# A decode step of two layers, twice: the row mean is carried by an extra column of wo and w2

## The chip, the cores and the metric

The kernel runs on one core of a Trainium2 chip. The metric is the device time of one execution in microseconds (us). The core has TensorE (PE in the profile; PEld is its weight load), VectorE (DVE), ScalarE (ACT), GpSimd (POOL) and SyncE (SP), which issues all transfers here.

## The reference

Eight batch rows, one token each, go through attention, a feed-forward part, the same attention again and the same feed-forward part again. Each has a residual and takes the normalised row:

```python
def _layernorm(x, axis=-1, eps=1e-5):
    m = jnp.mean(x, axis=axis, keepdims=True)
    v = jnp.var(x, axis=axis, keepdims=True)
    return (x - m) / jnp.sqrt(v + eps)
x = x + _A_ref(_layernorm(x), k_cache, v_cache, wq, wo)   # q = xn @ wq; softmax(q k^T / 16) v; @ wo
x = x + _B_ref(_layernorm(x), w1, w2)                     # silu(xn @ w1) @ w2
```

and so a second time. D is 448, there are 16 query heads and 8 key heads of 256, the last 1024 positions of K and V are used, and the hidden size of B is 1792. All is bf16. K and V of a batch are 8.4 MB, read once and kept for both attentions; the weights wq, wo, w1, w2 (3.7, 3.7, 1.6 and 1.6 MB) stay in SBUF.

The mean enters each product only through the row sums of the weights: (x - m) @ W is x @ W minus m times the column sums of W. The kernel before uses this; the change does not.

## The kernel before

**Order.** The kernel is a list of tasks, each with an engine, reads and writes (tiles and PSUM banks), an estimated duration and a priority. `Plan.schedule` plays them through in time with the constants at lines 12 to 30 (latencies, `OCC` durations by name, `HOLD`, `PE_SCALE`, and `BIAS`, which shifts the urgency of single kinds of task) and so fixes one order for each engine; `Plan.emit` writes it out with semaphore waits. Engines run their order strictly, so a task that waits holds everything behind it on its engine. SP's order is that in which the loads are listed.

**Loads.** x, wq, K of batch 0 (eight slots), wo, V of batch 0, w1, w2, then K and V of batches 1 to 7. There are 29 slots of 512 KB; a load into a used slot waits until the second attention has read it (`pump`). wo and w2 lie in SBUF as rows of 448 columns for each chunk of 128 input rows.

**Start** (`start_rows`, from line 522). x is turned into columns; the statistics of all 8 rows are taken (`stats8`); one product with wq gives all q of the first attention and, from a ninth column of ones (`xb0[:, :, NB]`, line 387), the column sums `csq`; these times the negative mean are added. `sums_w1` (line 558) gives w1's column sums `cs1` with 56 matmuls, once.

**One batch** (`layer1`, `layer2`). K is transposed in place on DVE (line 877, 16 operations), scores are 128 matmuls for both attentions (line 598), softmax follows. `x_init` (line 716) puts the residual row, as columns, in bank YB. P times V: four kv heads by rows (line 655), four by columns (line 684). `wo_part` (line 726) multiplies seven heads with wo into bank XB, four partial rows; `fold` (line 748) copies them with ACT (L750) and sums and turns them into columns in YB by five matmuls (`to_cols`, line 495), while two filler matmuls (`keep`, line 743) run on PE; the last head goes straight to columns (`wo_cols`, line 735). Then `chain` (line 755):

- `xcols`: DVE copies the row to `xbt` (L697). `stats`: four matmuls with ones give the sum (L701), four the sum of squares (L703); DVE makes nmean, vn, var4 (L706, L708, L711), POOL the power -1/2 (L713, `rhalf`).
- 56 matmuls with w1 (L488); DVE adds `cs1` times nmean (vpos, L762); ACT tanh (L766), DVE hT (L768); 14 matmuls with w2 (L771) into XB; `fold` again; `xcols` to `x2b` (L697); `stats` again.
- `maskr` on DVE (L779); two halves of q: 16 matmuls with wq (L784), copy on ACT (qrow, L789), turn (L792), qT2 on DVE with `csq` (L795), spread (L577) and masked (qbd, L581).

The second attention follows, beside the first attention of the next batch; its results of all batches wait in `oT2`. The end (`final_wo`, `final_rows`, from line 803) multiplies them with wo for all 8 rows, folds, takes `stats8`, w1, the `cs1` correction (L823, L826, L828), tanh and w2.

Of the kernel before, what the change touches and what calls it, by code (L numbers as in the profile page):

```python
# [18 lines left out]
OCC = {"dve:KT": 0.635, "dve:max": 0.35, "dve:maskr": 0.16, "dve:nmean": 0.10, "dve:vn": 0.15, "dve:var4": 0.15,  # L19
       "dve:vpos": 0.17, "dve:hT": 0.12, "dve:xb": 0.10, "dve:oTev": 0.10, "dve:qT2": 0.16, "dve:qbd": 0.36,  # L20
# [3 lines left out]
HOLD, PE_SCALE = 0.664, 1.032  # L24
BIAS = {"dve.KT.a": 22.4, "pe.S0.0.a": -78.2, "dve.max.a": 23.1, "pe.PV0.0.0.a": -52.9, "dve.oTev.a": 42.5,
        "pe.PV0.1.0.a": -21.9, "pe.PV0.1.1.a": 34.2, "dve.xb.b": 61.8, "dve.nmean.b": 76.2, "dve.vn.b": 130.7,
        "dve.var4.b": 69.1, "pe.w1.b": -131.8, "dve.vpos.b": 70.6, "dve.hT.b": 26.1, "dve.maskr.b": 46.5,
        "dve.qT2.b": 102.1, "dve.qbd.b": 99.0, "pe.S1.0.b": -54.5, "dve.max.b": 66.3, "dve.mT.c": 39.4,
        "pe.l.c": 48.6, "pe.PV1.0.0.c": 53.0, "pe.PV1.0.1.c": 55.7, "pe.PV1.0.2.c": 50.5, "pe.PV1.0.3.c": 51.6,
        "pe.oT.c": -34.2, "pe.PV1.1.1.c": 94.7, "pe.PV1.1.2.c": -48.5}  # L30
# [220 lines left out]
def bass_interleave_layers__sliding_block_cached__dense_activation_silu__decode_kernel(  # L251
# [18 lines left out]
    XC = 5  # L270

# [5 lines left out]
    wo_sb = sb("wo_sb", [P, NCH * D], BF16)  # L277
    w1_sb = sb("w1_sb", [P, 3 * F + F2], BF16)
    w2_sb = sb("w2_sb", [P, FC * D], BF16)
# [4 lines left out]
    deps_sb = sb("deps_sb", [P, 1], F32)  # L284
# [6 lines left out]
    xb0 = sb("xb0", [P, XC, NB + 1], BF16)  # L291
    x2b = sb("x2b", [P, XC, NB], BF16)
    csq = sb("csq", [P, NCH], F32)
    cs1 = sb("cs1", [P, FC], F32)
# [11 lines left out]
    nmean = sb("nmean", [P, 1], F32)  # L306
    vn = sb("vn", [P, 1], F32)
# [3 lines left out]
    rowb = qrow[:, 0:D]  # L311
    cols_b = sb("cols_b", [P, 3], BF16)
    ones4, zero_b = cols_b[:, 0:1], cols_b[:, 1:2]
    ones_b = cols_b[:, 2:3].broadcast_to([P, P])
    fold8 = sb("fold8", [P, NB], BF16)
    xbt = sb("xbt", [P, XC], BF16)
    vpos = sb("vpos", [P, FC], F32)
# [10 lines left out]
    big8 = e1f.bitcast(F32)  # L328
    z8 = q0f.bitcast(F32)[:, 0:FC * NB]
    th8 = e0f.bitcast(F32)[:, 0:FC * NB]  # L330
    hT8 = q1f[:, 0:FC * NB]
    xbt8 = sb("xbt8", [P, XC, NB], BF16)
    xrow = q1f[0:NB, 0:D]
# [6 lines left out]
    C_XF = 256  # L340
# [34 lines left out]
    dve(lambda e: e.memset(deps_sb[:], D * EPS), [], ["deps"], 0.08, -99)  # L375
# [11 lines left out]
    dve(lambda e: e.tensor_copy(xb0[:, :, NB], mask5[:]), M5, ["xb0_1"], 0.1, -98)  # L387
    for q in range(4):
        dve(lambda e, q=q: e.tensor_copy(fold8[32 * q:32 * q + 32, :], ident[32 * q:32 * q + 32, 32 * q:32 * q + NB]),
            ["ident"], [("fold8", q)], 0.08, -98)  # L390
        dve(lambda e, q=q: e.memset(mask[32 * q:32 * q + 32, :], 0.0), [], [("mask", q)], 0.08, -98)
        dve(lambda e, q=q: e.memset(mask[32 * q:32 * q + 32, q:q + 1], 1.0), [], [("mask", q)], 0.08, -98)
# [10 lines left out]
    SEL_R = [("sel", i) for i in range(4)] + [("mask", i) for i in range(4)]  # L403
# [23 lines left out]
    def load_wo():  # L427
        dma(lambda e: e.dma_start(wo_sb[:].rearrange("p (c n) -> p c n", n=D),
                                  A_wo.rearrange("(c p) n -> p c n", p=P)), ["wo"], HD * D * 2, "wo", rate=380e3)
# [71 lines left out]
    def stats8(xp, reads, prio):  # L501
# [7 lines left out]
               for c in range(KC)]  # L509
# [4 lines left out]
        dve(lambda e: e.tensor_scalar(nmean8, s1, -1.0 / D, None, op0=ALU.mult), bk(STB), [("qbd", 0, 1)], 0.17, prio)  # L514
        dve(lambda e: e.tensor_tensor(vn8, s1, nmean8, ALU.mult), bk(STB) + [("qbd", 0, 1)], [("qbd", 0, 1)], 0.17, prio)
        dve(lambda e: e.tensor_tensor(vn8, s2, vn8, ALU.add), bk(STB) + [("qbd", 0, 1)], [("qbd", 0, 1)], 0.17, prio)
        dve(lambda e: e.tensor_scalar(vn8, vn8, D * EPS, 4.0 / D, op0=ALU.add, op1=ALU.mult), [("qbd", 0, 1)], [("qbd", 0, 1)],
            0.12, prio)
# [3 lines left out]
    def start_rows(prio):  # L522
# [3 lines left out]
            for c in range(XC)], H8 + ["ident"], bk(YB), (NB, 1), prio)  # L526
        dve(lambda e: e.tensor_tensor(xb0[:, :, 0:NB], xp[:, 0:XC * NB].rearrange("p (c b) -> p c b", b=NB),
                                      mask5[:].unsqueeze(2).broadcast_to([P, XC, NB]), ALU.mult),
            bk(YB) + M5, ["xb0"], 0.2, prio)
        stats8(xb0[:, :, 0:NB], ["xb0"], prio)  # L530
        N9 = NB + 1
        pe(proj(YB, 0, range(NCH), wq_l, 16, lambda i: xb0[:, i, :], N9),
           ["xb0", "xb0_1"] + WQ_R, bk(YB), (N9, 1), prio, "q1")
        yv = bank[YB][:, 0:NCH * N9].rearrange("p (c n) -> p c n", n=N9)
        dve(lambda e: e.tensor_copy(csq[:], yv[:, :, NB]), bk(YB), ["csq"], 0.2, prio)
        t = big8.rearrange("p (c b) -> p c b", b=NB)
        dve(lambda e: e.tensor_tensor(t, csq[:].unsqueeze(2).broadcast_to([P, NCH, NB]),
                                      nmean8.unsqueeze(1).broadcast_to([P, NCH, NB]), ALU.mult),
            ["csq", ("qbd", 0, 1)], B8, 0.35, prio)
# [18 lines left out]
    def sums_w1(prio):  # L558
        pe(proj(STB, 0, range(FC), w1_l, 7, lambda i: xb0[:, i, NB:NB + 1], 1),
           ["xb0_1"] + W1_R, bk(STB), (CW, 1), prio, "cs1")  # L560
        dve(lambda e: e.tensor_copy(cs1[:], bank[STB][:, 0:FC * CW:CW]), bk(STB), ["cs1"], 0.2, prio)


    def q_blocks1(b, prio):
        for k2 in range(2):
# [5 lines left out]
                reads=[("q1s", b // 4)] + SEL_R, writes=[("qbd", 0, k2)], dur=0.65, prio=prio, name="qbd1")  # L571

    def q_blocks(layer, qi, k2, qrow, q_reads, prio):

        lb = LB[layer]
# [3 lines left out]
            sel[:, c, :], qrow.rearrange("p (k r a) -> p k a r", k=4, r=2), start=True, stop=True) for c in range(4)]  # L579
        pe(fns, q_reads + SEL_R, bk(lb), (16, 1), prio, "qsel")  # L580
        dve(lambda e: e.tensor_tensor(  # L581
            qbd[qi][:, 4 * k2:4 * k2 + 4, :, :].rearrange("p k c (q r) -> p (k c) q r", r=2),
            qs.rearrange("p (n r) -> p n r", r=2).unsqueeze(2).broadcast_to([P, 32, 4, 2]),
            maskr[:].unsqueeze(1).unsqueeze(3).broadcast_to([P, 32, 4, 2]), ALU.mult),
            bk(lb) + ["maskr"], [("qbd", qi, k2)], 0.43, prio, "qbd")
# [110 lines left out]
    def xcols(dst, key, prio):  # L696
        dve(lambda e: e.tensor_copy(dst, bank[YB][:, 0:XC]), bk(YB), [key], 0.17, prio, "xb")  # L697
# [248 lines left out]
```

## Time and profile before

| | |
|---|---|
| time of the runs | median 283.28 us of 3 (283.14 to 284.43) |
| the profiled execution | 283.31 us; its span 281.5 us |
| PE, PEld, DVE, ACT, POOL busy | 203.1, 119.2, 155.1, 51.4, 22.6 us |
| matmuls | 4406, as many weight loads |
| transfers | 78.29 MB, mean 278 GB/s |
| granted TensorE clock, mean | 0.859 |

The span is from the first to the last instruction. Busy time of PE contains the pipelining of matmuls; the chain of waits goes back from the last instruction, at each step to what released it. "issue" in it is time in which the engine waited for nothing that the profile shows. SPq is SP's own queue. L and a number is a line of the kernel before.

### The profile page before, as it was taken

To read this page: it belongs to the slowest core of one execution; us is meant where nothing else is said; L and a number is where in the kernel's file an instruction comes from. 1 tells how busy PE (TensorE), PEld (TensorE's weight loads), DVE (VectorE), ACT (ScalarE), POOL (GpSimd) and SP (SyncE) were. 2 spreads that over 40 slices of the span, in tenths; PEclk is the share of its full clock that TensorE was granted. 3 is DMA by queue.
4 is the path that set the end of the run, shared out by engine and by line. 5 is a ranking of instruction groups with operands and counts; after the bars stand their busy time and mean duration, and the time that the engine had idled before them with its cause. 6 is when DMAs were issued, how large, how long until landed. Compare 5 with 4: busy or idle time off the path is not lost.

```text
span 281.5 us, 9739 instructions
## 1 busy us (share of the span) xinstructions
PE 203.1 (72%) x4406; PEld 119.2 (42%) x4406; DVE 155.1 (55%) x480; ACT 51.4 (18%) x119; POOL 22.6 (8%) x41
## 2 busy tenths in 40 slices
PE   1040649686697977988787978789877987985853
PEld 0040315533363555356524643555354535743430
DVE  6279220187556947693777477646763766224122
ACT  2000020020321141214122202311231123221111
POOL 1200100020000200020010002000200020000020
PEclk9999975595797999799979978995898799999575
DMA  6999999999999499949995997799679956000000
GB/s 250 357 409 384 372 349 359 376 407 354 361 407 364 130 356 410 357 142 393 401 329 189 398 384 246 225 409 375 192 237 407 377 182 220 8 2 2 2 0 1
DMA packets 50153, 78.29 MB, mean 278 GB/s; under 512 B 2225, under 2 KB 41025, under 8 KB 49729
## 3 DMA queue, kind: packets, MB, share of 16 engines
q1 hardware_dynamic: 50112, 77.68, 77.7%
q8 instruction: 34, 0.56, 0.8%
q14 instruction: 7, 0.05, 0.0%
HBM read 77.67 MB, written 0.01 MB: 276 GB/s over the span
## 4 chain that ended last, share of the span: by engine, by line
PE 58%; SPq 14%; DVE 13%; issue 5%; ACT 4%; DMA 3%; POOL 1%; ACTq 0%; DVEq 0%
PE bank L655 9%; SPq L455 9%; PE bank L598 8%; PE bank L784 6%; PE bank L488 6%; PE bank L743 5%; PE bank L684 5%; PE bank L726 4%; PE bank L771 4%; DMA w_sb<-in_B_w_dram 3%; DVE mseg L604 3%; DVE slot L877 3%; SPq L449 2%; SPq L443 2%; PE bank L735 1%
## 5 line engine op out<-in xcount | busy, mean ns | idle before, releaser
L877 DVE STREAM_TRANSPOSE slot<-slot 128x512 uint32<-128x512 uint32 x128 | 84.9, 691 | 9.9 <-DMA slot<-in_A_k_cache_dram 9.4
L598 PE MATMUL bank<-slot,qbd 128*8 128x256 bf16 x1024 | 40.3, 299 | 7.3 <-DVE mg L611 4.1
L655 PE MATMUL bank<-slot,pT_sb 128*2 128x256 bf16 x768 | 28.3, 291 | 4.3 <-ACT pT_sb L627 3.4
L598 PEld LDWEIGHTS bank<-slot,qbd 128*8 128x8 bf16 x1024 | 22.9, 89 | 17.8 <-DVE mseg L604 5.2
L713 POOL TENSOR_TENSOR rhalf<-var,nhalf 128x1 f32<-128x1 f32 x16 | 8.7, 542 | 204.1 <-DVE var L711 204.1
L618 ACT ACTIVATE e_sb<-bank,mb 128x256 bf16<-128x256 f32 x32 | 14.1, 471 | 55.1 <-DVE mb L614 55.1
L743 PE MATMUL bank<-sel,cols_b 128*128 128x480 bf16 x56 | 21.4, 461 | 2.6 <-DVE vpos L762 2.6
L655 PEld LDWEIGHTS bank<-slot,pT_sb 128*2 128x2 bf16 x768 | 16.3, 86 | 10.7 <-ACT pT_sb L627 5.0
L690 DVE TENSOR_TENSOR oT<-bank,rl_sb 128x4 bf16<-128x4 f32 x32 | 5.2, 161 | 27.4 <-PE bank L684 27.4
L684 PEld LDWEIGHTS bank<-pT_sb,slot 128*128 128x128 bf16 x512 | 15.1, 98 | 11.0 <-issue 10.3
L684 PE MATMUL bank<-pT_sb,slot 128*128 128x2 bf16 x512 | 17.2, 164 | 3.6 <-issue 2.7
L604 DVE TENSOR_REDUCE mseg<-bank 128x1 f32<-128x256 f32 x32 | 13.5, 423 | 10.1 <-PE bank L598 9.0
L488 PE MATMUL bank<-xbt,w_sb 128*128 128x32 bf16 (+1 forms) x504 | 15.2, 180 | 5.0 <-issue 4.6
L784 PE MATMUL bank<-wq_sb,x2b 128*1 128x512 bf16 x256 | 16.9, 384 | 2.2 <-DVE x2b L697 2.2
L488 PEld LDWEIGHTS bank<-xbt,w_sb 128*128 128x128 bf16 x504 | 14.0, 99 | 5.5 <-issue 5.1
L726 PE MATMUL bank<-wo_sb,oT 128*1 128x448 bf16 x224 | 15.6, 420 | 0.5 <-DVE oT L668 0.3
L636 DVE TENSOR_REDUCE l_sb<-bank 128x16 f32<-128x64 f32 x16 | 3.5, 221 | 20.1 <-PE bank L631 20.1
L623 PE MATMUL bank<-ident,e_sb 128*128 128x128 bf16 x64 | 6.7, 232 | 10.9 <-ACT e_sb L618 10.9
L789 ACT ACTIVATE qrow<-bank 128x512 bf16<-128x512 f32 x16 | 9.6, 597 | 23.0 <-PE bank L784 14.6
L662 ACT ACTIVATE e_sb<-bank 128x256 bf16<-128x256 f32 x24 | 9.2, 383 | 22.2 <-PE bank L655 22.2
L566 POOL TENSOR_TENSOR qbd<-q1s,mask 128x256 bf16<-128x256 bf16 x16 | 9.8, 613 | 21.2 <-DVE q1s L554 20.0
L771 PE MATMUL bank<-w_sb,hT 128*1 128x448 bf16 x112 | 11.4, 502 | 0.0
(122 smaller groups left out, 190.0 us busy)
## 6 DMA issues: line engine op xcount, KB each, us to landing
slot<-in_A_k_cache_dram SPq DMA_DIRECT2D x64, 512.0 KB, 10.6
slot<-in_A_v_cache_dram SPq DMA_DIRECT2D x64, 512.0 KB, 9.3
wo_sb<-in_A_wo_dram SPq DMA_DIRECT2D x1, 3584.0 KB, 26.0
wq_sb<-in_A_wq_dram SPq DMA_DIRECT2D x3, 1024.0 KB, 6.8
w_sb<-in_B_w_dram SPq DMA_DIRECT2D x1, 1568.0 KB, 13.0
w_sb<-in_B_w_dram SPq DMA_DIRECT2D x1, 1344.0 KB, 11.5
wq_sb<-in_A_wq_dram SPq DMA_DIRECT2D x2, 256.0 KB, 10.0
w_sb<-in_B_w_dram SPq DMA_DIRECT2D x2, 112.0 KB, 10.0
```

The lines of the kernel that those rows point to most:

```text
L455: dma(lambda e: e.dma_start(slots[s][:, :].rearrange("v (j n) -> v j n", j=4), src.rearrange("j (v uh) d -> v j (uh d)", uh=2)), [("slot", ...
L488: fns.append(lambda e, o=o, i=i, r=r: e.matmul(bank[bank_i][:, col + (o - outs[0]) * n:col + (o - outs[0] + 1) * n], lhs(o, i), r.broadcas ...
L598: fns.append(lambda e, cb=cb, par=par, j=j, kvh=kvh, kv=kv: e.matmul(bank[sc][32 * j:32 * j + 8, k2 * 256:(k2 + 1) * 256], qbd[qi][:, kvh, ...
L604: dve(lambda e: e.tensor_reduce(mseg[layer][:, k2:k2 + 1], bank[sc][:, k2 * 256:(k2 + 1) * 256], AX.X, ALU.max, negate=True), bk(sc), [("m ...
L618: act(lambda e, k2=k2: e.activation(e_sb[ei][:, k2, :, :].rearrange("p uh (jj ul) -> p uh jj ul", ul=4), bank[sc][:, k2 * 256:(k2 + 1) * 2 ...
L655: fns.append(lambda e, q=q, uh=uh, j=j, vv=vv: e.matmul(bank[ob][32 * j:32 * j + 2, c0:c0 + DH], pT_sb[ei][:, k2 * 2 + uh, j * 8 + 2 * q:j ...
L684: fns.append(lambda e, a=a, q=q, uh=uh: e.matmul(bank[vb][:, c0 + 2 * a:c0 + 2 * a + 2], vs[:, (2 * q + uh) * DH + a * P:(2 * q + uh) * DH ...
L726: fns.append(lambda e, i=i, c=c, kvh=kvh: e.matmul(bank[XB][32 * c:32 * c + 1, 0:D], oT1[:, i % 2, i // 2:i // 2 + 1], wo_sb[:, i * D:(i + ...
L743: pe([lambda e: e.matmul(bank[YB][:, 32:512], zero_b.broadcast_to([P, P]), sel[:].rearrange("p c m -> p (c m)")[:, 0:480], start=False, st ...
L771: pe([lambda e, f=f: e.matmul(bank[XB][32 * (f % 4):32 * (f % 4) + 1, 0:D], hT[:, f:f + 1], w2_sb[:, f * D:(f + 1) * D], start=(f < 4), st ...
L784: pe([lambda e, j=j, c=c, k2=k2, wb=wb: e.matmul(bank[wb][32 * j:32 * j + 1, :], x2[:, xcol(c, k2):xcol(c, k2) + 1], wq_sb[:, c * HD + ((4 ...
L877: dve(lambda e, v=v: e.transpose(v, v), [("slot", s)], [("slot", s)], 0.67, prio, "KT")
```

## The change

wo and w2 get a row pitch of 450 columns in SBUF (`DP`); column 448 holds minus the row sum over 448. `row_sums` makes it on the chip after the weights have landed: groups of rows in turn on DVE (one reduce of 4 or 5 rows and a scale) and on ACT (one copy with an accumulated sum for each row, and a copy). All products with wo wait for wo's eight groups, all with w2 for w2's four. w2 is loaded ahead of wo instead of behind w1.

The partial rows so have a 449th column, the negative mean of what is folded in. A sixth matmul of `to_cols` spreads it over all partitions into column 5 of YB; `wo_cols` gets four matmuls for it and `x_init` a second one with the low part of the mean (`xl0`). `xcols` adds that column to the row and masks it, in one operation of DVE, so `xbt` is centred. The sum matmuls, nmean, vn, vpos, `cs1`, `csq` and `sums_w1` go; var4 is an activation, as are maskr and a copy that keeps the row and its mean in `x2b`; the scale 2/16 moves into `mask`. tanh and hT read w1's bank. The second filler pair writes XB and reads wq. In the start, x is centred and split in a high and a low part (16 columns for q in place of 9, summed by one reduce). In the end the mean is a bf16 column (`nm8`), added and masked by two operations; the correction shrinks to one multiplication, and one matmul puts the mean back. The planner's constants are new.

```diff
-HOLD, PE_SCALE = 0.664, 1.032
-BIAS = {"dve.KT.a": 22.4, ...
+HOLD, PE_SCALE = 0.368, 1.013
+BIAS = {"pe.S0.0.a": -30.6, "dve.max.a": -4.8, "pe.PV0.0.2.a": -33.7, "pe.wo.a": 11.0, "pe.PV0.1.1.a": 56.1,
+        "pe.PV0.1.2.a": 10.4, "pe.keep.b": -44.7, "pe.wq.b": 14.6, "act.qrow.b": -18.2, "pe.S1.0.b": -29.4,
+        "dve.mT.c": -116.1, "pe.l.c": -24.2, "pe.oT.c": -8.5, "pe.PV1.1.0.c": -30.8, "pe.PV1.1.3.c": 37.4,
+        "pe.wo8.c": -80.4}
...
     def load_w2():
-        dma(lambda e: e.dma_start(w2_sb[:].rearrange("p (c n) -> p c n", n=D),
+        dma(lambda e: e.dma_start(w2_sb[:].rearrange("p (c n) -> p c n", n=DP)[:, :, 0:D],
...
-    WO_R = ["wo"]
-    W2_R = ["w2"]
+    WO_R = ["wo"] + [("wo_s", g) for g in range(8)]
+    W2_R = ["w2"] + [("w2_s", g) for g in range(4)]
+
+    def row_sums(w, key, groups, prio):
+
+        for g, (i0, i1) in enumerate(groups):
+            n = i1 - i0
+            row = sums[:, (8 if key == "w2" else 0) + g, :]
+            view = w[:, i0 * DP:i1 * DP].rearrange("p (c n) -> p c n", n=DP)
+            if g % 2 == 0:
+                dve(lambda e, view=view, n=n, row=row: e.tensor_reduce(row[:, 0:n], view[:, :, 0:D], AX.X, ALU.add,
+                                                                       negate=True),
+                    [key], [("sums", key, g)], 1.94, prio, "rsum")
+                dve(lambda e, view=view, n=n, row=row: e.tensor_scalar(view[:, :, D], row[:, 0:n], 1.0 / D, None,
+                                                                       op0=ALU.mult),
+                    [("sums", key, g)], [(key + "_s", g)], 0.15, prio)
+            else:
+                for i in range(i0, i1):
+                    act(lambda e, i=i, i0=i0, row=row: e.activation(
+                        qrow[:, 0:D], w[:, i * DP:i * DP + D], ACTF.Copy, scale=-1.0 / D,
+                        accum_out=row[:, i - i0:i - i0 + 1]), [key], ["rowb", ("sums", key, g)], 0.75, prio, "rsum")
+                act(lambda e, view=view, n=n, row=row: e.activation(view[:, :, D], row[:, 0:n], ACTF.Copy),
+                    [("sums", key, g)], [(key + "_s", g)], 0.22, prio)
...
+        fns.append(lambda e: e.matmul(bank[bank_i][:, col + XC * nb:col + (XC + 1) * nb],
+                                      row[:, D:D1].broadcast_to([P, P]), rhs, start=False, stop=True,
+                                      skip_group_check=True))
         pe(fns, reads, bk(bank_i), shape, prio, name)
...
-    def xcols(dst, key, prio):
-        dve(lambda e: e.tensor_copy(dst, bank[YB][:, 0:XC]), bk(YB), [key], 0.17, prio, "xb")
...
+    def xcols(prio):
+        dve(lambda e: e.scalar_tensor_tensor(out=xbt[:], in0=bank[YB][:, 0:XC], scalar=bank[YB][:, XC:XC + 1],
+                                             in1=mask5[:], op0=ALU.add, op1=ALU.mult), bk(YB) + M5, ["xbt"], 0.23, prio,
+            "xb")
+
+    def stats(bi, col, prio):
+        s2 = bank[bi][:, col:col + 1]
+        pe([lambda e, c=c: e.matmul(s2, xbt[:, c:c + 1].broadcast_to([P, P]), xbt[:, c:c + 1],
                                     start=(c == 0), stop=(c == KC - 1)) for c in range(KC)],
...
+        act(lambda e: e.activation(var4[:], s2, ACTF.Identity, bias=eps4[:, 0:1], scale=4.0 / D), bk(bi) + ["eps4"],
+            ["var4"], 0.25, prio, "var4")
...
+        for i in range(4 * kvh, 4 * kvh + 4):
+            fns.append(lambda e, i=i: e.matmul(
+                bank[YB][:, XC:XC + 1], wo_sb[:, i * DP + D:i * DP + D1].broadcast_to([P, P]),
+                oT1[:, i % 2, i // 2:i // 2 + 1], start=False, stop=True, skip_group_check=True))
...
-        dve(lambda e: e.scalar_tensor_tensor(out=vpos[:], in0=cs1[:], scalar=nmean[:, 0:1], in1=y1,
-                                             op0=ALU.mult, op1=ALU.add),
-            bk(YB) + ["cs1", "nmean"], ["vpos"], 0.23, prio, "vpos")
-        keep(2, prio)
-        act(lambda e: e.activation(th[:], vpos[:], ACTF.Tanh, scale=rhalf[:, 0:1]), ["vpos", "rhalf"], ["th"], 0.31,
+        act(lambda e: e.activation(th[:], y1, ACTF.Tanh, scale=rhalf[:, 0:1]), bk(YB) + ["rhalf"], ["th"], 0.31,
             prio, "tanh")
+        keep(2, prio, XB)
...
+        xcols(prio)
+        act(lambda e: e.activation(x2b[:, :, b], bank[YB][:, 0:XC + 1], ACTF.Copy), bk(YB), [("x2b", b)], 0.25, prio,
+            "x2b")
+        stats(LB[1], C_ST, prio)
+        act(lambda e: e.activation(maskr[:], mask[:], ACTF.Copy, scale=rhalf[:, 0:1]), ["rhalf"] + MASK_R, ["maskr"],
+            0.22, prio, "maskr")
...
+            dve(lambda e, k2=k2: e.tensor_copy(qT2[:, 16 * k2:16 * k2 + 16], bank[lb][:, C_QT:C_QT + 16]),
...
+        dve(lambda e: e.tensor_copy(nm8[:], x8[:, XC * NB:]), bk(YB), ["nm8"], 0.17, prio)
+        xcf = big8[:, 0:XC * NB].rearrange("p (c b) -> p c b", b=NB)
+        dve(lambda e: e.tensor_tensor(xcf, x8[:, 0:XC * NB].rearrange("p (c b) -> p c b", b=NB),
+                                      nm8[:].unsqueeze(1).broadcast_to([P, XC, NB]), ALU.add), bk(YB) + ["nm8"], B8, 0.22,
+            prio)
+        dve(lambda e: e.tensor_tensor(xbt8[:], xcf, m58, ALU.mult), B8 + M5, ["xbt8"], 0.2, prio)
...
-        dve(lambda e: e.tensor_tensor(t, cs1[:].unsqueeze(2).broadcast_to([P, FC, NB]),
-        dve(lambda e: e.tensor_tensor(z, t, bank[XB][:, 0:FC * NB].rearrange("p (f b) -> p f b", b=NB), ALU.add),
-            bk(XB) + B8, Z8, 0.25, prio + 0.2)
...
             if x == (0, "k", 7):
+                load_w2()
                 load_wo()
             if x == (0, "v", 7):
                 load_w1()
-                load_w2()
...
+        if b == 0:
+            row_sums(w2_sb, "w2", [(0, 4), (4, 7), (7, 11), (11, 14)], 40)
+            row_sums(wo_sb, "wo", [(0, 5), (5, 8), (8, 13), (13, 16), (16, 21), (21, 24), (24, 29), (29, 32)], 40)
...
-        if b == 0:
-            sums_w1(0)
```

More of the change, by code (lines that the diff above doesn't have):

```diff
@@ L18 @@
        "sp": {"pe": 0.05, "dve": 0.07, "act": 0.05, "pool": 0.06, "sp": 0.1}}
-OCC = {"dve:KT": 0.635, "dve:max": 0.35, "dve:maskr": 0.16, "dve:nmean": 0.10, "dve:vn": 0.15, "dve:var4": 0.15,
-       "dve:vpos": 0.17, "dve:hT": 0.12, "dve:xb": 0.10, "dve:oTev": 0.10, "dve:qT2": 0.16, "dve:qbd": 0.36,
+OCC = {"dve:KT": 0.635, "dve:max": 0.35, "dve:hT": 0.17, "dve:xb": 0.16, "dve:oTev": 0.10, "dve:qbd": 0.36, "dve:rsum": 2.3, "dve:qT2": 0.12,
+       "act:maskr": 0.13, "act:var4": 0.16, "act:x2b": 0.16, "act:rsum": 0.66,
        "act:exp": 0.38, "act:oev": 0.30, "act:pTev": 0.20, "act:qrow": 0.51, "act:rowb": 0.50, "act:tanh": 0.22,
```

210 lines of the change are left out of this document (95 added, 115 removed).

## The prediction

> **What bounds the kernel now.** I read the page first, then the stretches between the starts of successive batches' w1 products, then the chain of waits in order of time.
>
> ```profile
> span 281.5 us, 9739 instructions
> PE 203.1 (72%) x4406; PEld 119.2 (42%) x4406; DVE 155.1 (55%) x480; ACT 51.4 (18%) x119; POOL 22.6 (8%) x41
> GB/s 250 357 409 384 372 349 359 376 407 354 361 407 364 130 356 410 357 142 393 401 329 189 398 384 246 225 409 375 192 237 407 377 182 220 8 2 2 2 0 1
> q8 instruction: 34, 0.56, 0.8%
> L877 DVE STREAM_TRANSPOSE slot<-slot 128x512 uint32<-128x512 uint32 x128 | 84.9, 691 | 9.9 <-DMA slot<-in_A_k_cache_dram 9.4
> ```
>
> By stretch (length, then busy us of PE, PEld, DVE, ACT, POOL, granted clock, DMA share, GB/s):
>
> ```profile
> 0.00:52.00 52.00, 19.67 (x423) 12.67 (x424) 22.95 (x83) 4.15 (x8) 4.24 (x11) 0.87 1.01 353
> 112.30:139.00 26.70, 22.32 (x508) 13.22 (x509) 17.87 (x53) 5.93 (x14) 2.57 (x5) 0.94 0.90 321
> 192.90:221.60 28.70, 23.94 (x517) 13.78 (x518) 17.83 (x53) 5.93 (x14) 2.31 (x4) 0.84 0.86 304
> ```
>
> The first 52 us are transfers (DMA share 1.01). A later batch takes 26.7 to 28.7 us; PE is busy 22 to 24 of them and the DMA share is below one, so the order on PE and its waits set the pace. From the chain of waits (start, length, what):
>
> ```profile
> 85.27 1.04 issue
> 111.31 1.22 issue
> 112.54 1.21 PE bank L488 x41
> 113.77 0.24 DVE vpos L762
> 115.04 1.59 PE bank L771 x13
> 132.35 0.16 DVE oT L690
> 132.85 0.93 PE bank L684 x31
> 133.78 1.43 PE bank L726 x28
> 136.30 0.65 PE bank L735 x20
> 137.98 1.16 issue
> 139.14 1.14 PE bank L488 x39
> 164.34 1.16 issue
> 186.24 1.09 issue
> 214.25 1.59 issue
> 249.35 0.94 PE bank L771 x14
> ```
>
> Two things are to be seen. The mean correction stands on this path as vpos (0.24), and in the statistics matmuls. And PE stands still for 1.0 to 1.6 us in each of batches 1 to 6 for nothing that the profile names ("issue"), 7.3 us in six rows. In batches 2 and 3 it comes with 41 and 39 of the 56 w1 matmuls left, that is every 508 matmuls or so. PE's 8812 instructions over the 34 packets of the instruction queue are 259 to a packet, so I read it as a wait for PE's next instructions, at every fourth packet. After the stop the w2 matmuls take 1.59 us; in batch 7, with no stop and no traffic, 0.94.
>
> **The change, part by part.** Durations are from this execution: 283.31 us, 1.8 us more than its span; the median of the runs is 283.28.
>
> ```profile
> L706 DVE TENSOR_SCALAR nmean<-bank 128x1 f32<-128x1 f32 x16 | 2.3, 144 | 4.0 <-PE bank L703 4.0
> L708 DVE SCALAR_TENSOR_TENSOR vn<-bank,nmean,deps_sb 128x1 f32<-128x1 f32 x16 | 3.5, 219 | 0.6
> L711 DVE TENSOR_SCALAR var<-bank,vn 128x1 f32<-128x1 f32 x16 | 3.5, 219 | 0.6
> L762 DVE SCALAR_TENSOR_TENSOR vpos<-cs,nmean,bank 128x14 f32<-128x14 f32 x8 | 1.8, 229 | 7.4 <-PE bank L488 7.3
> L766 ACT ACTIVATE th<-vpos,rhalf 128x14 f32<-128x14 f32 x8 | 2.5, 307 | 38.0 <-DVE vpos L762 38.0
> L779 DVE TENSOR_SCALAR maskr<-mask,rhalf 128x4 f32<-128x4 f32 x8 | 3.6, 445 | 0.0
> L697 DVE CAST xbt<-bank 128x5 bf16<-128x5 f32 x8 | 1.3, 161 | 4.6 <-PE bank L735 4.6
> ```
>
> *Per batch, on the path.* vpos goes: tanh starts on the w1 bank, and the two filler matmuls, now on the other bank, no longer wait for it, -0.27 with its hop. One-column matmuls cost 0.65/20 = 0.033. Four statistics matmuls go twice (-0.26); one comes in each fold (+0.07), four in the wo columns (+0.13), one in x_init (+0.03). Centring turns the cast of 161 ns into an operation of vpos's kind, 229, twice (+0.14). wo and w2 rows of 449 columns instead of 448: nothing. Sum -0.16, for eight batches -1.3. The row mean buys little there because it trades matmuls for matmuls on the engine that sets the pace.
>
> *Per batch, beside the path.* DVE loses nmean, vn and var4 twice (1.16 us), vpos and maskr (0.67), and gains 0.14; its 17.9 us of 26.7 become about 16.2. ACT takes var4 twice, maskr and x2b. None is seen on ACT in this form: between the 0.14 of nmean and the 0.45 of maskr; I take 0.3, tanh's 0.307 being nearest, so 1.2 us on an engine busy 5.93 of 26.7. What is queued behind them on ACT are the two qrow copies of the second attention's q, for which PE's turns wait; against that, rhalf's chain is shorter by nmean and vn (0.36). It evens out: zero on the path, up to 0.3 if maskr goes ahead of qrow. qT2 becomes a plain copy, some 0.05 less, uncounted. A lighter DVE makes waits behind a K transpose (0.69) rarer, by between none and one a batch; I take 0.1, near none, since PE is mostly not waiting: -0.8.
>
> *The start.*
>
> ```profile
> wo_sb<-in_A_wo_dram SPq DMA_DIRECT2D x1, 3584.0 KB, 26.0
> 8.61 0.90 SPq L428
> 41.95 9.55 DMA w_sb<-in_B_w_dram
> 51.63 3.16 PE bank L488 x112
> 55.89 0.87 PE bank L771 x14
> 72.62 1.88 PE bank L598 x23
> L604 DVE TENSOR_REDUCE mseg<-bank 128x1 f32<-128x256 f32 x32 | 13.5, 423 | 10.1 <-PE bank L598 9.0
> L636 DVE TENSOR_REDUCE l_sb<-bank 128x16 f32<-128x64 f32 x16 | 3.5, 221 | 20.1 <-PE bank L631 20.1
> L750 ACT ACTIVATE qrow<-bank 128x448 bf16<-128x448 f32 x8 | 4.3, 543 | 30.3 <-PE bank L726 30.3
> ```
>
> On SP's queue w2 (1792 rows of 896 B, 1.6 MB) now passes wo, V of batch 0 and w1. At 384 GB/s each of those lands 4.2 us later, K of batch 1 as before. wo landed at 8.61 + 26.0 = 34.6, now 38.8. Its row sums: the two reduces give 1.05 ns an element, so five rows take 2.5 us and DVE's four groups 10 us, until 48.8; w2's two take 4 us before that; ACT's 18 rows at 0.54 are 10 us. Their cover is the transfers: DVE idles 29 and ACT 48 of the first 52 us, and the V of batch 0 comes behind wo on the queue, with w1 last, at 51.5 + 4.2 = 55.7. Without it the wo products of batch 0 would slip by up to 10 us.
>
> Behind w1 the 56 column-sum matmuls go (half of 3.16), so batch 0's w2 product starts near 57.9 instead of 55.89: 2.0 us late. That is hidden: the first scores of batch 1 at 72.62 wait for its K transposes, sixteen of 0.69 on DVE, whose K lands as before, with batch 0's chain worked off in between. That chain is lighter by a nmean, a vn, a var4 and a maskr, 1.0 us. I take -1.0; without the cover +1.0. In the setup, centring x, splitting it in two and a reduce in place of two adds are some 0.2 us operations while PE waits for wq: zero. The row pitch of wo and w2 (900 B for 896) might slow 5.3 MB: between nothing and the step from 409 to 349 GB/s, 2.2 us; I take +0.5, near nothing, since the pieces stay 896 B long.
>
> [...]
>
> *The end.*
>
> ```profile
> L826 DVE TENSOR_TENSOR qbd<-e_sb,bank 128x112 f32<-128x112 f32 x1 | 0.3, 270 | 0.0
> ```
>
> Three small statistics operations of nmean's kind go (-0.5 with hops) and two of three 112-column ones (-0.6); two 40-column ones come, between 0.16 (xbt's 5 columns) and 0.27 (112), nearer the first (+0.4 with hops); four one-column matmuls go, one comes (-0.1). Sum -0.8.
>
> *The stops of PE.* Batch 1 is reached 56 matmuls earlier, and each batch has one fewer. So the packet boundary that lay about 15 matmuls into w1 lies 55 to 65 later: behind w1, in the w2 product or the fold. The old packet from the oT step at 132.35 to the stop at 137.98 lasted 5.6 us and needed 6.8. The new one, shifted, loses 31 of L684 (0.93) and most of the wo rows (1.2), gains the rest of w1 (1.14), the fillers with tanh (0.9) and part of w2 (0.6): 6.1 us, in later batches up to 7. That leaves stops of 0.7, 0.5 and 0.2, then none. The packet before it was late in L684 by 1.09 and 1.59 in batches 5 and 6; it now ends in the wo rows, which PE takes more slowly (1.43 for 28 against 0.93 for 31): I take 0.7 in each of six batches. 5.6 in place of 7.3: -1.7. The bounds are the two rivals below. This assumes that the new plan keeps PE's order, which its new biases leave open.
>
> [...]
>
> Sum: -1.3 - 0.8 - 1.0 + 0.5 - 0.8 - 1.7 = -5.1, against 283.3: 278.2.
>
> **The rivals.**
>
> *The stops vanish.* A stop with its slow clock costs 1.2 + (1.59 - 0.94) = 1.8 us. If no packet is late at its new place, six of these go, -10.8 instead of -1.7: 269.1. For it: the boundary meets slower work than w1. Against: two packets remain shorter than what they needed.
>
> *The stops get worse (slower).* If the packet that ends in the wo rows is late in every batch, all run like 192.9 to 221.6: 28.7 us at clock 0.84 instead of 26.7. Four more batches pay 2.0, and a stop behind w1 adds to some: +9, with -3.4 from the rest: 289. It decides where that packet lacks about 1 us, more than my 0.7. For it: the two stops in L684 had this cost. Against: the wo rows are slower.
>
> *Nothing is gained.* The removed DVE work lies off the path, ACT's operations hold qrow for 0.3 a batch (+2.4), and batch 0's lateness shows (+2.0): 282.6.
>
> **How the numbers follow.** Forecast 0.48 (own range 276 to 281), vanish 0.17, nothing 0.17, worse 0.18. A change under 0.5% cannot be told from none, so faster means below 281.9: 0.17, 0.43 of the forecast's 0.48 and a little of the third, 0.62. Same 0.20, slower 0.18. The range leaves out the far halves of the outer cases: 271 to 287.
>
> **What would show it.** In the new profile: nmean, vn and vpos gone and tanh released by PE; DVE 1.7 us lighter a batch; batch 0's w2 product near 58 and batch 1's first scores near 71.6; the "issue" pieces at most 1 us, behind w1 or in the wo rows; 0.8 less from the last fold to the end. I am wrong if the issue pieces sum to under 2 or over 10 us, if batch 1's scores start after 73, or if PE waits for ACT's var4 or maskr.

## The result, and the profile after

The changed kernel takes 276.54 us (the median of four runs, three of 274.94 to 277.37 and one of 285.92), the kernel before 283.86 us beside it: a ratio of 0.9722, with a 95% interval of 0.9655 to 0.979. Each ratio here is against runs of the kernel before on the same chip and leaves out slow runs, those more than 1.5% above the fastest run of the same kernel. The changed kernel was run and profiled a second time beside later experiments (276.2 us in that profile).

The profiled execution takes 274.94 us with a span of 273.2, against 283.31 and 281.5. Its page, with the busy time of each engine and the granted clock in 40 slices:

```profile
span 273.2 us, 9613 instructions
PE 196.6 (72%) x4340; PEld 116.6 (43%) x4340; DVE 153.9 (56%) x427; ACT 70.5 (26%) x193; POOL 22.6 (8%) x41
PEclk9999999999979999799979997997999799979575
```

DVE is hardly lighter, 153.9 for 155.1, because the row sums cost 14 us of what the batches save. The span is 8.3 us shorter, and by the starts of the batches' w1 products it divides so: batch 1's w1 starts at 86.12 in place of 84.82 (+1.3); from there to batch 7's w1 it takes 152.8 us in place of 162.0 (-9.2); from there to the end 34.3 in place of 34.65 (-0.4). Stretch n is from batch n's w1 to that of batch n+1, with the second attention of the one and the first of the other. Stretches 1 to 5 of the changed kernel (length, then busy us of PE, PEld, DVE, ACT, POOL, granted clock, DMA share, GB/s):

```profile
86.10:111.40 25.30, 21.19 (x506) 13.18 (x507) 17.62 (x48) 6.77 (x18) 2.31 (x4) 1.00 0.93 328
111.40:136.70 25.30, 22.06 (x505) 13.18 (x505) 16.06 (x46) 6.77 (x18) 2.31 (x4) 0.93 0.91 324
136.70:162.75 26.05, 21.68 (x505) 13.19 (x506) 16.00 (x46) 6.77 (x18) 2.31 (x4) 0.93 0.95 331
162.75:188.55 25.80, 22.14 (x505) 13.19 (x505) 15.99 (x46) 6.77 (x18) 2.31 (x4) 0.93 0.95 337
188.55:214.10 25.55, 21.41 (x505) 13.10 (x505) 15.95 (x46) 6.77 (x18) 2.31 (x4) 0.94 0.94 330
```

And stretch 4 of the kernel before, which with stretch 5 (28.6 us, clock 0.84, shown in the prediction) was the slowest:

```profile
163.80:193.10 29.30, 23.98 (x509) 13.68 (x507) 18.09 (x53) 5.93 (x14) 2.31 (x4) 0.81 0.89 319
```

None of the changed kernel's stretches falls under 0.93 in clock, and 6.5 of the 9.2 us come out of stretches 4 and 5 alone (29.3 to 25.8, 28.6 to 25.55). The chain of waits of the changed kernel shows what became of PE's stops:

```profile
40.57 2.36 issue
42.94 7.26 DVE e_sb L444 x3
50.34 0.58 PE bank L710 x16
...
58.69 1.51 PE bank L508 x56
60.83 1.50 PE bank L794 x13
...
157.73 1.43 PE bank L749 x28
159.42 1.21 issue
...
184.96 0.55 PE bank L749 x8
185.87 0.67 issue
...
210.73 0.46 PE bank L710 x15
211.19 1.00 issue
...
261.23 0.56 ACT qrow L837
...
270.75 0.61 DVE e_sb L869
```

Three stops of 2.9 us in all lie on this chain, in stretches 3 to 5 (ahead of the w1 of batches 4 to 6), behind the wo rows (L749) or in the PV columns that follow (L710). Before, six took 7.3. PE's own rows show two more beside the chain: 0.21 us ahead of batch 3's w1, and 0.64 us in the wo rows ahead of batch 2's w1, where the chain waits for a load of K:

```profile
108.53 0.35 PE L749 MATMUL bank<-wo_sb,oT 128*1 128x449 bf16 x1 [0.64 <-issue]
```

So PE stood still for 3.7 us in these batches, and only batches 1 and 7 had no stop. The piece at 40.57 is none of these: it lies within the first of wo's four row sums on DVE, which run from 40.53 to 50.2 and are on the chain.

### The profile page after: what moved, and what is told of

The parts are those of the page before. It is cut to its first block, busy times and chain, and to the rows that moved or that the text cites. A ratio compares the mean times of both kernels' runs of the same rounds, so it can differ in the third digit from the quotient of the medians.

```text
span 273.2 us, 9613 instructions
## 1 busy us (share of the span) xinstructions
PE 196.6 (72%) x4340; PEld 116.6 (43%) x4340; DVE 153.9 (56%) x427; ACT 70.5 (26%) x193; POOL 22.6 (8%) x41
## 4 chain that ended last, share of the span: by engine, by line
PE 53%; DMA 18%; DVE 14%; SPq 5%; issue 4%; ACT 4%; POOL 1%; ACTq 0%; DVEq 0%
DMA wo_sb<-in_A_wo_dram 11%; PE bank L624 8%; PE bank L681 7%; DMA slot<-in_A_k_cache_dram 7%; PE bank L808 6%; PE bank L508 5%; PE bank L770 5%; PE bank L710 4%; PE bank L749 4%; PE bank L794 4%; DVE slot L901 3%; DVE e_sb L444 3%; SPq L463 2%; DVE mseg L630 2%; PE bank L602 1%
## 5 line engine op out<-in xcount | busy, mean ns | idle before, releaser
L901 DVE STREAM_TRANSPOSE slot<-slot 128x512 uint32<-128x512 uint32 x128 | 82.7, 688 | 8.8 <-DMA slot<-in_A_k_cache_dram 8.7
L624 PE MATMUL bank<-slot,qbd 128*8 128x256 bf16 x1024 | 37.9, 283 | 10.7 <-DVE mseg L630 8.8
L681 PE MATMUL bank<-slot,pT_sb 128*2 128x256 bf16 x768 | 29.3, 298 | 11.9 <-DMA slot<-in_A_v_cache_dram 8.8
L710 PE MATMUL bank<-pT_sb,slot 128*128 128x2 bf16 x512 | 17.2, 164 | 5.8 <-issue 3.1
L770 PE MATMUL bank<-wq_sb,cols_b 128*128 128x480 bf16 x56 | 20.7, 447 | 0.4 <-ACT var L732 0.4
L710 PEld LDWEIGHTS bank<-pT_sb,slot 128*128 128x128 bf16 x512 | 14.9, 97 | 12.1 <-issue 9.9
L808 PE MATMUL bank<-wq_sb,xbt 128*1 128x512 bf16 x256 | 16.6, 378 | 2.6 <-DVE xbt L723 2.6
L630 DVE TENSOR_REDUCE mseg<-bank 128x1 f32<-128x256 f32 x32 | 12.6, 412 | 7.7 <-PE bank L624 6.9
L749 PE MATMUL bank<-wo_sb,oT 128*1 128x449 bf16 x224 | 14.2, 379 | 0.7 <-issue 0.6
L794 PE MATMUL bank<-w_sb,hT 128*1 128x449 bf16 x112 | 11.9, 519 | 0.9 <-DVE hT L791 0.6
L732 ACT ACTIVATE var<-bank,eps 128x1 f32<-128x1 f32 x16 | 4.2, 262 | 31.0 <-PE bank L729 31.0
L649 PEld LDWEIGHTS bank<-ident,e_sb 128*128 128x128 bf16 x64 | 4.0, 104 | 18.9 <-ACT e_sb L644 17.1
## 6 DMA issues: line engine op xcount, KB each, us to landing
w_sb<-in_B_w_dram SPq DMA_DIRECT2D x1, 1344.0 KB, 11.2
```

What stands on the lines that cost most here:

```text
L624: fns.append(lambda e, cb=cb, par=par, j=j, kvh=kvh, kv=kv: e.matmul(bank[sc][32 * j:32 * j + 8, k2 * 256:(k2 + 1) * 256], qbd[qi][:, kvh, ...
L630: dve(lambda e: e.tensor_reduce(mseg[layer][:, k2:k2 + 1], bank[sc][:, k2 * 256:(k2 + 1) * 256], AX.X, ALU.max, negate=True), bk(sc), [("m ...
L649: pe([lambda e, c=c: e.matmul(bank[lb][:].bitcast(BF16)[:, c * P:(c + 1) * P], e_sb[ei][:, c // 2, c % 2, :], ident[:, :], is_transpose=Tr ...
L681: fns.append(lambda e, q=q, uh=uh, j=j, vv=vv: e.matmul(bank[ob][32 * j:32 * j + 2, c0:c0 + DH], pT_sb[ei][:, k2 * 2 + uh, j * 8 + 2 * q:j ...
L710: fns.append(lambda e, a=a, q=q, uh=uh: e.matmul(bank[vb][:, c0 + 2 * a:c0 + 2 * a + 2], vs[:, (2 * q + uh) * DH + a * P:(2 * q + uh) * DH ...
L749: fns.append(lambda e, i=i, c=c, kvh=kvh: e.matmul(bank[XB][32 * c:32 * c + 1, 0:D1], oT1[:, i % 2, i // 2:i // 2 + 1], wo_sb[:, i * DP:i ...
```

## The experiments

The first question was whether the stops follow the cut of PE's program into the packets of its instruction queue, and whether the change gained by shifting that cut. In the profile of the kernel before the stops ahead of the w1 of batches 1 to 4 lie 509, 508 and 509 matmuls apart, each at the fourth packet after the last, so a packet holds 127 matmuls with their weight loads; the expectations round this to 128, or 256 instructions. Spare matmuls at the start, where PE waits for wq, move the cut for all that follows and leave the order of the tasks alone: the first four matmuls of the q1 product are repeated.

### The same kernels, cut elsewhere

In the changed kernel, with 56, 12, 112 and 32 spare matmuls (n / 4 = 14, 3, 28, 8), and in the kernel before with 72:

```diff
     pl.schedule()
+    q1 = [t for t in pl.order["pe"] if t.name == "q1"][0]
+    q1.fns = q1.fns[:4] * 14 + q1.fns
     pl.emit()
```

> The changed kernel with 56 spare matmuls added at the start, where PE waits for wq, so that the same order of work stands 56 matmuls later in PE's packets of 256 instructions. Every fourth packet then begins 0 to 20 matmuls into w1 again, as before the change, and the one ahead of it 2 to 22 matmuls into the PV columns. If the packet boundaries caused the gain, the stops come back: 5 to 7.5 us of issue pieces in batches 1 to 6 in place of 2.9, and 279 to 283 us. If the gain is the work that was taken off PE's and DVE's path, and the stops are by chance, the time stays within 0.5% of 276.5.

Measured: 289.1 us, ratio 1.014 (1.0077 to 1.0202); span 286.0, 9.8 us of issue pieces in eight rows, clock 0.881: more than was expected. With the cut where the kernel before had it the changed kernel is slower than the kernel before, though it does the same work as the changed one.

> The kernel before, unchanged but for 72 spare matmuls at the start (the same as 56 fewer, for packets of 128 matmuls). Every fourth packet then begins in the w2 product or in the fold, and the one ahead of it in the last ten of the 28 wo rows or just behind them, as in the changed kernel. If the boundaries caused most of the gain: at most 3 us of issue pieces in place of 7.3, and 276 to 279 us. If the removed work did: 283, with stops of about 1 us at the new places.

Measured: 282.8 us, ratio 0.9951 (0.991 to 0.9992); span 281.0. A miss for both: the stops went to the new places and stayed about as long, 6.65 us in batches 1 to 6 and 1.61 in batch 0. Its chain of waits:

```profile
83.15 1.04 PE bank L726 x19
84.19 1.02 issue
...
111.23 1.21 issue
...
137.86 1.39 issue
...
164.70 0.85 issue
...
191.31 1.09 issue
...
217.32 1.09 issue
```

So the place alone does not decide. In this kernel a cut in the wo rows or just behind them stops PE for 0.85 to 1.39 us in every batch; in the changed kernel it did not in batch 1, and for 0.64 us in batch 2.

> The changed kernel with 12 spare matmuls at the start. The boundary of the packet that in batches 3 to 5 lay 2 to 10 matmuls into the last PV columns, with stops of 1.21, 0.67 and 1.00 us, then lies in the wo rows up to batch 5, where batches 1 and 2 had no stop. If a stop is set by what work stands at the boundary: under 1 us of issue pieces in batches 1 to 5, and 274 to 275.5 us. If a stop comes wherever the queue is late: as many as before, 276.5.

Measured: 280.8 us, ratio 0.9874 (0.9816 to 0.9933); span 277.7, stops of 1.17, 1.89 and 0.94 us, the longest in the wo rows, where none was expected. A miss.

> The changed kernel as it is, beside the next three on one chip, so that they can be compared with it. Its ratio to the kernel before should again be within 0.9655 to 0.979. If its few stops were luck of that chip, they come in more batches here, 4 to 7 us in place of 2.9, and the time rises by about 1.75 us for each us of them (the slope between the profiles so far: 273.2 with 2.9 us, 286.0 with 9.8).

Measured: six runs of 274.95 to 281.73 us, four of them at 279.6 or more; their median, 279.7, is 1.5% under the 284.0 of the kernel before beside it, where the first set had 2.6%. The span of the profile is 274.4, with 3.95 us of issue pieces in four rows, which is more than in the first profile of the same kernel.

> The changed kernel with 112 spare matmuls at the start. Cut this way, no packet of 128 matmuls is shorter than 5.3 us from batch 2 on, where it is 4.6 to 5.2 as the kernel stands; the arrival of a packet takes some 5.5 to 6.2 us from the start of the one before it. If a stop is that time less what the running packet lasts: under 1.5 us of issue pieces in batches 1 to 6, and the fastest of these kernels, 270 to 273 us as a span. If a stop depends on which work stands at the boundary and not on the packet's length: no better than the unpadded one.

Measured: 276.8 us, ratio 0.9742 (0.9696 to 0.9787); span 274.5, clock 0.943, 4.8 us of issue pieces, one of them 2.44. A miss: the long packets did not remove the stops; the packet behind the longest could run only 8.5 us after it was asked for.

> The changed kernel with 32 spare matmuls at the start: the worst cut, two packets of 4.3 to 5.5 us in each batch. By packet length: 9 to 11 us of issue pieces in batches 1 to 6 and a span of 284 to 288 us. If the position alone decides (the boundary is in the middle or at the end of w1 and at the first wo rows): about 1 us a batch, 280.

Measured: 292.4 us, ratio 1.0256 (1.0192 to 1.0319); span 290.4, clock 0.893. Its chain of waits has 11.1 us of issue pieces, two for most batches, at a cut behind the PV columns or in the wo rows and at a cut in w1:

```profile
108.32 0.81 PE bank L710 x27
109.13 1.10 issue
...
114.82 0.64 PE bank L508 x25
115.46 0.69 issue
...
193.53 0.48 PE bank L749 x7
194.01 1.48 issue
...
199.68 0.94 PE bank L508 x37
200.62 1.06 issue
```

32 matmuls of 0.03 us, done while PE waits for wq, cost 16 us against the second profile of the unpadded kernel, and 12.7 us by the medians of all runs (292.4 and 279.7).

The trace's records of the instruction queue give the working of a stop. They hold when each packet started and how long it took. The cuts are counted from the stops, one for every 127 matmuls. That a packet is asked for when PE enters the one before it is a reading of the light kernels below: there a packet starts within 2.0 us of that moment, mostly within 0.8. In the profiles of the kernel before and of the changed one, under load, it starts up to 4.1 us after that moment and takes 0.93 to 1.31 us (68 packets), and after a stop of batches 1 to 6 PE goes on 1.3 to 1.5 us after its end. In the table, "asked" is the time at which PE enters the packet before, and "can run" is the end of the packet and 1.4 us. Times in us, with the batch whose w1 comes next (the light kernel is of an experiment below):

```
kernel, batch              asked   starts  can run  PE is there  stop
changed, 1 (wo rows)       78.76    80.33    82.81        83.69  none
changed, 2 (wo rows)      102.95   106.06   108.51       107.89  0.64
changed, 6 (PV columns)   206.22   209.79   212.28       211.17  1.00
before + 72, 2 (wo rows)  106.33   109.98   112.27       111.05  1.21
changed + 32, 2 (PV col.) 104.55   107.82   110.30       109.11  1.10
changed + 32 light, 2     100.77   101.25   103.84       105.32  none
```

Between asking and start lie 1.6 to 3.7 us in the rows under load, so a packet can run 4.0 to 6.1 us after it was asked for; the 127 matmuls of PV columns, wo rows and w1 last 4.6 to 5.2 us.

### Loads taken away

If that is so, the stops must go when K and V are light, wherever the cut lies. From batch 2 on the loads of K and V bring an eighth and a quarter of their bytes; tasks, order and all instructions stay, and the attention of batches 2 to 7 is computed on older data.

```diff
     def load_k(s, b, kvh):
+        u1 = 8 if b < 2 else 1
...
-                                  A_k_cache[b, kvh, S0:SK, :].rearrange("(p u) d -> p u d", p=P)),
+                                  A_k_cache[b, kvh, S0:SK, :].rearrange("(p u) d -> p u d", p=P)[:, 0:u1, :]),
     def load_v(s, b, g):
+        q1 = 4 if b < 2 else 1
```

> The kernel before, with the loads of K and V from batch 2 on cut to an eighth and a quarter of their bytes (the rest of each slot keeps older data, so the attention of batches 2 to 7 is computed on it; every instruction on the engines stays). If the stops of PE are its instruction packets waiting behind K and V on the DMA queues, no issue piece over 0.3 us is left from batch 3 on though the boundaries lie as before, and the batches take about 25 us instead of 25.3 to 29.4: some 265 to 270 us. If the stops belong to the place in the program, they stay.

Measured: 269.8 us, ratio 0.9517 (0.9456 to 0.9578); span 267.7 and no stop left.

> The changed kernel with K and V cut in the same way. Without stops the difference to the light kernel before is what the change itself does to the work: by the terms of the sum -0.16 on the path and -0.1 for the lighter VectorE, -0.26 us a batch, some -1.5 us over batches 2 to 7. If the whole gain of -9.2 us over six batches is work, 1.5 us a batch.

Measured: 267.6 us, ratio 0.9421 (0.935 to 0.9492); span 265.0, no stop in the batches.

> The changed kernel with 32 spare matmuls at the start, with K and V cut in the same way. With full loads these 32 matmuls cost 5%. If they do so by the late packets alone, this one is within 0.5% of the light changed kernel; if by where they put other work, it stays slower by some 5%.

Measured: 266.8 us, ratio 0.9422 (0.9359 to 0.9485); span 263.5, no stop in the batches. The 32 matmuls that cost 5% cost nothing here. So the stops are late packets, and it is the transfers of K and V that make them late: with those cut to an eighth and a quarter of their bytes, none is left of the 7.3, 2.9 and 11.1 us that the three kernels have under full loads.

By the medians the change is worth 2.2 us where no packet is late (269.8 to 267.6, with intervals that overlap) and 7.3 us with full loads (283.86 to 276.54). So by these medians the larger part of the gain comes only with full loads, where it depends on how the packets meet them.

The light kernels also weigh the work without stops. Stretches 2 and 3 of the light kernel before, then of the light changed one, columns as above:

```profile
109.35:134.43 25.08, 21.82 (x512) 13.18 (x509) 17.60 (x53) 5.94 (x14) 2.31 (x4) 0.93 0.24 66
134.43:158.60 24.17, 20.82 (x512) 13.00 (x509) 17.62 (x53) 5.94 (x14) 2.31 (x4) 1.00 0.24 69
```

```profile
110.63:134.51 23.88, 20.57 (x505) 13.08 (x505) 15.76 (x46) 6.76 (x18) 2.31 (x4) 1.00 0.26 69
134.51:158.33 23.82, 20.57 (x506) 13.08 (x506) 15.79 (x46) 6.76 (x18) 2.30 (x4) 1.00 0.25 69
```

At full clock a batch takes 24.17 against 23.82: the change saves 0.35 us. But four of the six stretches of the light kernel before contain 3.4 us at half clock and take 25.0 to 25.1 us; none of the light changed kernel does. The six together take 148.76 us and 143.06, so 5.7 us less without any stop, 2.1 of it work (six times 0.35) and 3.6 clock. The half clock does not come in every run: one of the four runs of the light kernel before has a clock of 0.947, that of the light changed kernel, and takes 267.5 us. At 160.48 of the light kernel before PE has stood 0.33 us for vpos ahead of the two fillers; in the light changed kernel the fillers follow w1 at once. That this short wait is what lets the clock drop was not tried apart.

### The cut held still

With 505 matmuls a batch and a cut at every 509 (the changed kernel's stops ahead of the w1 of batches 4, 5 and 6 lie 509 apart) the cut moves by four from batch to batch; four more matmuls make the batch 509 too, which the expectation counts as 512. Here it is held where the trace of the changed kernel had no packet under 5.7 us:

```diff
+    q1.fns = q1.fns[:4] * 26 + q1.fns
+    for t in [t for t in pl.order["pe"] if t.name == "xinit"][2:]:
+        t.fns = t.fns[:1] * 4 + t.fns
```

> The changed kernel with full loads, 104 spare matmuls at the start and four more in each of batches 2 to 7 (x_init repeated), so that a batch is 512 matmuls long and every batch is cut at the same four places, for which no packet was shorter than 5.7 us in the trace. Waits of a packet of up to 6.2 us then leave stops of at most 0.5 us each, 2 us in all, at some 1.5 us for the spare matmuls: 271 to 274 us as a span. If packets come later when PE is faster, since K and V are then asked for sooner, the stops stay at 3 to 5 us and nothing is gained.

Measured: 278.5 us, ratio 0.9856 (0.9793 to 0.9919). Its profile is of its fastest run (274.5 us, span 272.7) and has three stops, in every second batch:

```profile
108.67 1.85 issue
...
160.00 1.86 issue
...
211.35 1.85 issue
```

There the packet starts 4.7 to 4.8 us after it was asked for, in the batches between 3.2, and PE is through the packet before it in 5.3 to 5.5 us, not 5.7. So the rival holds: the cut that was good in one trace was not in the next. No version that was run beats the changed kernel beyond the intervals.

### The start

> The changed kernel with wo ahead of w2 on the queue and w2's row sums behind wo's. wo lands near 36.4 instead of 40.5 us, its sums end near 46 instead of 50.2, and batch 0's oT step, whose input was there at 47.87, is not held any more. If the row sums are on the chain of the start, batch 0's w1 starts 1 to 2.3 us earlier than 58.48 and the time is 274.5 to 276. If batch 1 waits for its K anyway, its w1 starts at 86 as now and the time is 276.5.

```diff
-                load_w2()
                 load_wo()
+                load_w2()
...
-            row_sums(w2_sb, "w2", [(0, 4), (4, 7), (7, 11), (11, 14)], 40)
             row_sums(wo_sb, "wo", ...)
+            row_sums(w2_sb, "w2", [(0, 4), (4, 7), (7, 11), (11, 14)], 59)
```

Measured: 281.3 us, ratio 0.9828 (0.9764 to 0.9892); span 278.9 with 6.6 us of stops. Batch 0's w1 starts at 57.52 in place of 58.48, when w1 has landed, and batch 1's at 86.95: the 1.0 us is not passed on. The row sums are on batch 0's chain, but batch 1 waits for its K.

> The kernel before with rows of wo and w2 kept at 900 B in place of 896 (two small buffers are moved to make room for them); order, row sums and all else as before. If the pitch slows the load: wo lands later than 34.6 us, by 1.5 to 5 us (in the changed kernel it took 31.0 us from issue with 1.6 MB more ahead of it, against 26.0; at 384 GB/s those account for 4.2), and w1 later than 51.5 by 1.5 to 2.2. If only the order moved it: 34.6 and 51.5 as before, and no difference in time.

```diff
-    wo_sb = sb("wo_sb", [P, NCH * D], BF16)
+    wo_sb = sb("wo_sb", [P, NCH * 450], BF16)
-    w2_sb = sb("w2_sb", [P, FC * D], BF16)
+    w2_sb = sb("w2_sb", [P, FC * 450], BF16)
```

(with the slices of both, and th and xbt8 moved into qrow and q1s). Measured: 284.5 us, ratio 1.0005 (0.9972 to 1.0038). The load of wo, and the first K transpose of batch 1, which waits for its load:

```profile
wo_sb<-in_A_wo_dram SPq DMA_DIRECT2D x1, 3584.0 KB, 27.5
```

```profile
58.57 0.71 DVE L877 STREAM_TRANSPOSE slot<-slot 128x512 uint32<-128x512 uint32 x1 [1.66 <-DMA slot<-in_A_k_cache_dram]
```

wo takes 27.5 us for 26.0 and batch 1's w1 starts at 86.79 for 84.82, yet the time is the same: by batch 2's w1 (110.88 for 110.79) it is made up, because stretch 1 has neither its stop of 1.04 us nor the 3.4 us of half clock of the kernel before. The pitch costs 1.2 to 1.6 us at the start.

## Why the prediction was right, and where not

The time (278.2 forecast, 276.54 measured) lies in the forecast's own range, but two terms of the sum, the start and the stops, were mis-sized in opposite directions, and the slow clock was left out of it. That these nearly cancel is luck, and so is the place of the cut: the same kernel's second set of runs has a median of 279.7.

*Work per batch, -0.26 us (-0.16 on the path, -0.1 for a lighter DVE): right.* The light kernels give -0.35 at full clock, and DVE is 1.8 us lighter there (17.62 to 15.79). vpos is gone and tanh is released by PE. ACT's added operations do little harm: PE waits for them once, 0.35 us for var4 in batch 0, which the prediction had named as a sign of being wrong. Their groups in the changed kernel:

```profile
L732 ACT ACTIVATE var<-bank,eps 128x1 f32<-128x1 f32 x16 | 4.2, 262 | 31.0 <-PE bank L729 31.0
L803 ACT ACTIVATE maskr<-mask,rhalf 128x4 f32<-128x4 f32 x8 | 2.4, 298 | 1.4 <-POOL rhalf L734 1.4
L800 ACT ACTIVATE x2b<-bank 128x6 bf16<-128x6 f32 x8 | 1.6, 198 | 7.1 <-DVE xbt L723 7.1
L444 DVE TENSOR_REDUCE e_sb<-wo_sb 128x5 f32<-128x2240 bf16 x4 | 9.7, 2480 | 4.0 <-DMA wo_sb<-in_A_wo_dram 4.0
L452 ACT ACTIVATE qrow<-wo_sb 128x448 bf16<-128x448 bf16 x12 | 6.9, 576 | 5.1 <-DMA wo_sb<-in_A_wo_dram 4.8
L452 ACT ACTIVATION_READ_ACCUMULATOR qrow<-wo_sb 128x1 f32 x12 | 2.2, 187 | 0.0
```

0.20 to 0.30 each, for 0.3 taken. The two reduces gave the row sums' price well (2.48 for 2.5); the sums on ACT cost 0.76 a row for 0.54, since each is followed by a read of the accumulator.

*The start, -1.0 + 0.5: +1.3.* Here the DVE rows of batch 1's K transposes, first and last (the reduce that follows them). Before:

```profile
56.94 0.71 DVE L877 STREAM_TRANSPOSE slot<-slot 128x512 uint32<-128x512 uint32 x1 [1.27 <-DMA slot<-in_A_k_cache_dram]
...
72.48 0.12 DVE L611 TENSOR_REDUCE mg<-mT 128x2 f32<-128x8 f32 x1
```

After:

```profile
58.30 0.71 DVE L901 STREAM_TRANSPOSE slot<-slot 128x512 uint32<-128x512 uint32 x1 [1.26 <-DMA slot<-in_A_k_cache_dram]
...
72.85 0.72 DVE L630 TENSOR_REDUCE mseg<-bank 128x1 f32<-128x256 f32 x2
```

From the first transpose to the end of the last it takes 14.6 us in place of 15.5: the -1.0 was right. But the first K lands 1.4 us later. "K of batch 1 as before" and "I take +0.5" for the 900 B pitch failed; the pitch alone does it (1.6 in its experiment). There wo's packets were in transfer for 12.6 us in place of 11.6, 9% longer. The other 0.9 us appear by the end of batch 1's PV rows, into which 3.4 us of half clock fall now (75.6 to 79.1; before, 72.6 to 76.0, mostly ahead of them). The cover named for the row sums held only in part: they end at 50.2 (48.8 was forecast) and hold batch 0's oT step from 47.9 on. w2's product starts at 60.83 and not near 57.9; moving wo's row sums forward gained 1.0 us of that, and w1, which landed near 57.5 and not at 55.7, accounts for most of the rest.

The prediction called the scores at 72.62 batch 1's first; they are its last 32 matmuls, which wait for the last K transposes. In the changed kernel they come 1.0 us later, past the 73 that was named as a sign of being wrong, 0.4 because the transposes end later and 0.6 because two maxima of DVE (the L630 row above) now stand between the last transpose and them:

```profile
73.62 1.05 PE L624 MATMUL bank<-slot,qbd 128*8 128x256 bf16 x32 [2.52 <-DVE mseg L630]
```

*The end, -0.8: right.* From the last fold's copy to the last copy the kernel before has

```profile
268.79 0.55 ACT qrow L815
...
279.07 0.61 DVE e_sb L845
```

10.28 us, the changed kernel (261.23 to 270.75) 9.52: -0.76. From batch 7's w1 to the last w1 product it is 0.9 us longer, with 10.2 us at half clock for 6.8, so only 0.4 of the end shows in the span.

*The stops, 5.6 in place of 7.3: 2.9, or 3.95 in the second profile.* The mechanism was right: the cut at the place named, no stop there, and the remaining stops at the tail of the wo rows, 1.21 us at most. What was mis-sized is "I take 0.7 in each of six batches" and the price. The step compared packet lengths with a need of 6.8 us, as if the arrival were fixed. For the packet behind the wo rows it is 4.0 to 6.3 us in the changed kernel's profile, and a packet of another run took 8.5. (The 6.8 itself was counted from the oT step; from the cut, at 132.9, it was 6.3.) And the main sum counted the bare stop, 1.7 us, though the rival priced a stop with its slow clock. How the 9.2 us divide is not settled. 4.4 are stops on the chain and 2.1 are work (six times 0.35). The clock records of the two traces hold 34.1 us at half clock in the six stretches before and 17.1 after (11.2 and 9.3 in stretches 4 and 5 before, 3.7 and 3.2 after); 3.4 us of it cost 0.9 (25.08 against 24.17), so 17 us fewer give 4.5, an estimate and not a run. The three make 11.0, more than there is, so they overlap or the clock is priced too high. By the light kernels, 5.7 us of such a difference need no stop, which leaves 3.5 for the late packets. And another run divides otherwise: in the second profile of the changed kernel the six stretches take 157.5 us, 27.3 of them at half clock, in place of 152.8, and what follows takes 30.9 in place of 34.3.

So the rival "the stops vanish" holds a part of the gain, at most about half, and "the stops get worse" was near: with 32 or 56 matmuls more ahead of batch 0 the changed kernel measured above the kernel before, 1.0256 and 1.014.

What stays open: why this packet waits only 1.6 to 3.1 us in the changed kernel's batches 1 to 3, and 3.1 to 3.6 at the same cut of the kernel before. The author's guess is the transfers of that moment, which no run held fixed; two profiles of one kernel differ by 1 us of stops.

## What to carry to other kernels

Before a gain of 2 or 3% is put down to an edit, run the same kernel with its program shifted by a few dozen idle instructions: here that alone moved the time from 0.972 to 1.026 of the kernel before. Weigh the edit's own work with the stops taken away (light loads, the same instructions). Here a packet's matmuls ran for 4.6 to 5.2 us where the next packet could run only 4.0 to 6.1 us after it was asked for, and K and V cut to an eighth and a quarter of their bytes took the stops away. Fewer or longer instructions, or the same bytes with less of them queued at once, were not tried. A better place for the cut was no remedy: held where one trace had no packet under 5.7 us, it stopped PE for 1.85 us in every second batch of the next.

## What the runs showed of the hardware

A packet of PE's instructions, 127 matmuls with their weight loads, started at most 2.0 us after PE entered the packet before it with light loads; with full ones mostly 2.5 to 4.1 us and at most 5.9 us after. That it is asked for at that moment is a reading: in the profiles before and after none started more than 0.2 us ahead of it. It took 0.93 to 1.31 us, and after a stop of batches 1 to 6 PE went on 1.3 to 1.5 us after its end. In the clock records of the two profiles the granted clock falls to half for 3.4 us or a multiple of it (3.4, 6.8, 10.2 or 17.1 us; the last record, at the end of the span, aside). It did so beside stops of 1.0 to 1.9 us, and four times in the light kernel before with no stop, so what lets it drop was not isolated. A row sum by ScalarE's accumulator cost 0.187 us for the read beside 0.576 (L452 of the changed kernel).
